# The fourth granule's x transposed by the DMA queue, and its FFN half moved back

## The chip, the core and the metric

The kernel runs on one core of a Trainium2 chip. The metric is the device time of one execution in microseconds; the median of several runs counts. Of the core's engines these notes speak of TensorE (PE; its weight loads are listed apart as PEld), VectorE (DVE), ScalarE (ACT), GpSimd (POOL) and SyncE (SP). SyncE computes nothing: it issues transfers to the core's 16 DMA engines, as GpSimd and ScalarE can too.

## What is computed

Attention over 4 batches, 8 heads, 768 positions and a head width of 64, with a window of 96 positions, 8 global positions and a bias by distance; then a feed-forward network with a scaled squared ReLU on the 3072 tokens of width 512.

```python
scores = q @ k.T / sqrt(64) - slope[h] * dist        # masked: kept if global or local
a = softmax(scores)
x = (a @ v), heads side by side                      # 3072 x 512
h = x @ w_in                                         # 3072 x 2048
g = s * relu(h) ** 2 + b
out = g @ w_out                                      # 3072 x 512
```

## The kernel before

The tokens are cut into twelve granules of 256 (three for each batch; j = 0 to 11), and each granule's attention into four units of two heads, so unit u belongs to granule u // 4. These notes count granules from 1 in words: the fourth is j = 3. (Where a number follows the word granule, as in granule 3, it is j.)

For a granule the work runs like this. GpSimd loads k, q and v (`load_granule`, L110 to L117; `load_qk`, `load_v`), cast to bf16 on the way. q and k are transposed: by TensorE for j = 0 to 3 (`qk_first`, `qk_block`, `qk_wide`), and by SyncE's queue, four transfers a granule, for j from 4 on (`qk_by_dma`, L356, issued at L360). `stage_S` makes a unit's scores on TensorE (L441), ScalarE takes the exponential (L450), VectorE multiplies by the mask (L457). `stage_A` multiplies by v (L495) and VectorE normalises into `xn` (L465, L466). Then `xn` has to be transposed into `xT`: `x_by_pe` (L583) does it with eight transposes of TensorE (L591) and two copies out of PSUM (L594), one of VectorE and one of ScalarE; `x_by_dma` (L596) does it with two transposing transfers of SyncE (L599). `finish_granule` (L950) takes the first for j below `X_PE`, which is 4. Behind it, it sends GpSimd a small copy that reads the end of `xT[j]` (`hold_loads`, L120, the copy is L122), and behind that copy the loads of granule j + 4: the loads wait in GpSimd's queue until `xT[j]` is there.

The FFN has two halves. The first (`p1_mm`, L612; matmuls at L619) takes two blocks of 128 hidden columns at a time, so eight groups `fp` of eight matmuls a granule; ScalarE applies the ReLU into `gT` (L629) and VectorE squares it (L632). The second half for the first four granules is `p2_mm` (L662; L667): for each of two output tiles `tb` of 128 tokens sixteen matmuls over the hidden blocks, which can be cut into ranges. `p2_out` adds the bias and stores through SyncE (L687). Later granules go in pairs through `product` (L819), a form with seven products for eight.

The order of the work on every engine is written by hand (`manual_schedule`): each engine takes its instructions in the order in which the lines run. Lines 1010 to 1143 are an opening, written line by line, up to granule 3's attention and x. From L1149 on the order comes from `step(s, c0, c1, c2)` (L959). Step s issues the transposes of granule j + 2 where its turn is (j = s // 2), emits the scores of step s + 1 with their exponentials and masks, then the list c0, the attention product of unit 2s, the list c1, that of unit 2s + 1, and the list c2; at a granule's second step it calls `finish_granule` after the first entry of c2. `flush` emits what was put off in `outs`. Step 8 and step 9 work on granule 4's attention and fill in FFN work: the second output tiles of granule 2 and the first half of granule 3 (`late_p1(3, ...)`). Step 10 begins the w_out tiles of granule 3.

In the opening, each head has a diagonal matrix (`diagonal`, L230), by which TensorE adds the bias of the first granules to the scores (L416, L517). ScalarE makes all eight (L232): four at L234, ahead of its cast of the first q (L260), and four at L1013, ahead of its copy of q's transposes (L331).

Of the kernel before, what the change touches and what calls it, by code (L numbers as in the profile page):

```python
# [17 lines left out]
def kernel(  # L18
# [13 lines left out]
    nc = tc.nc  # L32
    P = nc.NUM_PARTITIONS

    B, H, S, D = q.shape
# [9 lines left out]
    FC = DF // P  # L45
# [7 lines left out]
    QSCALE = 1.0 / float(D) ** 0.5  # L53
# [11 lines left out]

    ctx.enter_context(tc.manual_schedule())
    QK_PE = 4
    X_PE = 4
    LEAD = 4
    BIAS_PE = 2  # L70
    SHIFT = 6
# [112 lines left out]
    ident_bf = const.tile([P, P], BF16, name="ident_bf")  # L184
# [42 lines left out]
    slopes = [float(2.0 ** (-8.0 * (h + 1) / H)) for h in range(H)]  # L227
    diag = open_bf[:, 3 : 3 + H, :]

    def diagonal(hs):  # L230
        for h in hs:
            nc.scalar.activation(diag[:, h, :], ident_bf[:], ACT.Copy, scale=slopes[h] / QSCALE)  # L232

    diagonal(range(0, 4))  # L234

    tmpl = const.tile([P, H, 6, P], BF16, name="tmpl")

# [58 lines left out]
    def attach(b, lo, hi):  # L296

        kx = qk[b][0]
        nc.vector.tensor_copy(
            kx[:, lo:hi, :, P : P + NG],  # L300
            kx[:, 0, :, 0:NG].unsqueeze(1).to_broadcast((P, hi - lo, HP, NG)),
        )
# [53 lines left out]
    def qk_by_dma(j):  # L356
        b, g = divmod(j, NGR)
        for i in range(GB):
            for n in range(2):
                nc.sync.dma_start_transpose(  # L360
                    qk_of(b, n)[:, g * GB + i],
                    nat[j][:, n, i, :, :].rearrange("p h d -> p (h d)"),
                )
# [12 lines left out]
    def make_koff(j, blocks=range(GB)):  # L376
        b, g = divmod(j, NGR)
        if g == 0 or j >= SHIFT:
            return
        kx, ko = qk[b][0], koff_of(j)  # L380
        i0, n = blocks[0], len(blocks)
        lo = g * GB - 1 + i0
        nc.vector.tensor_copy(ko[:, i0 : i0 + n], kx[:, lo : lo + n, :, 0:P])
        nc.vector.tensor_copy(
            ko[:, i0 : i0 + n, :, 0:NG],
            kx[:, 0, :, 0:NG].unsqueeze(1).to_broadcast((P, n, HP, NG)),
        )
# [83 lines left out]
    def stage_A(u, pool=None):  # L471
        j, hp, b, g = unit(u)
        first = g == 0
        pt = st.pop(u)
        vn = vbuf[b % 2]
        if pool is None:
            av = ps_av.tile([P, GB, 2, VW], F32, name="ps_av", tag="av")
        else:
            av = pool.tile([P, GB, 2, VW], F32, name="ps_av2", tag="psh")
        if j not in xn:  # L480
            xn[j] = xpool.tile([P, GB, DM], BF16, name="xn", tag="xn")
        if first:
            dcol, ocol = ((0, 1), (None, 2)) if j < BIAS_PE else ((1, 2), (None, 0))
        else:
            dcol, ocol = (0, 3), (1, 2)
        for i in range(GB):
            for hi in range(2):
                h = 2 * hp + hi
                terms = [(dcol[i], vn[:, g * GB + i, h, 0 : D + 1])]
                if not first:  # L490
                    terms.append((ocol[i], voff_of(j)[:, i, h, 0 : D + 1]))
                elif i == 1:
                    terms.append((ocol[i], vn[:, 0, h, 0 : D + 1]))
                for n, (c, vv) in enumerate(terms):
                    nc.tensor.matmul(  # L495
                        av[:, i, hi, 0 : D + 1],
                        lhsT=pt[:, hi, c * P : (c + 1) * P],
                        rhs=vv,
                        start=(n == 0),
                        stop=(n == len(terms) - 1),  # L500
                    )
        normalize(
            xn[j][:, :, 2 * hp * D : (2 * hp + 2) * D].rearrange("p i (h d) -> p i h d", d=D), av
        )
# [78 lines left out]
    def x_by_pe(j, evac=(nc.vector.tensor_copy, nc.scalar.copy)):  # L583
        t = xT_tile(j)
        nk = KC // len(evac)
        for e, ev in enumerate(evac):
            ps = ps_h.tile([P, nk, GT], BF16, name="ps_x", tag="psh")
            for kc in range(nk):
                for i in range(GB):
                    c = (e * nk + kc) * P  # L590
                    nc.tensor.transpose(  # L591
                        ps[:, kc, i * P : (i + 1) * P], xn[j][:, i, c : c + P], ident_bf[:]
                    )
            ev(t[:, e * nk : (e + 1) * nk, :], ps[:])  # L594
# [6 lines left out]
    def g_of(j):  # L601

        if j // 2 not in gT:
            gT[j // 2] = gpool.tile([P, FC, 2 * GT], BF16, name="gT", tag="gT")
        return gT[j // 2][:, :, (j % 2) * GT : (j % 2 + 1) * GT]
# [6 lines left out]
    def p1_mm(j, fp):  # L612

        g = g_of(j)
        ps = ps_h.tile([P, 2, GT], F32, name="ps_1", tag="psh")
        for i in range(2):
            fc = 2 * fp + i
            for kc in range(KC):
                nc.tensor.matmul(  # L619
                    ps[:, i, :],  # L620
                    lhsT=w_in_bf[:, kc, fc * P : (fc + 1) * P],
                    rhs=xT[j][:, kc, :],
                    start=(kc == 0),
                    stop=(kc == KC - 1),
                )
        gs = g[:, 2 * fp : 2 * fp + 2, :]

        def relu():
            nc.scalar.activation(gs, ps[:], ACT.Relu)  # L629

        def square():
            nc.vector.tensor_tensor(gs, gs, gs, ALU.mult)  # L632

        return relu, square
# [27 lines left out]
    def p2_mm(j, tb, lo=0, hi=FC):  # L662
        if lo == 0:
            po_cur[j, tb] = ps_h.tile([P, DM], F32, name="ps_2", tag="psh")
        po = po_cur[j, tb]
        for fc in range(lo, hi):
            nc.tensor.matmul(  # L667
                po[:],
                lhsT=g_of(j)[:, fc, tb * P : (tb + 1) * P],
                rhs=w_out_bf[:, fc, :],  # L670
                start=(fc == 0),
                stop=(fc == FC - 1),
            )
# [34 lines left out]
    def moe_p2(j, tb):  # L708
        p2_mm(j, tb)
        outs.append(lambda: p2_out(j, tb))  # L710

    def flush():
        while outs:
            outs.pop(0)()
# [209 lines left out]
    def late_p1(j, fps):  # L924

        def go(fp):
            relu, square = p1_mm(j, fp)
            relu()
            outs.append(square)

        return [lambda fp=fp: go(fp) for fp in fps]

    p1 = {j: [lambda j=j, f=f: moe_p1(j, f) for f in range(FC // 2)] for j in range(NJ)}
    p2 = {j: [lambda j=j, t=t: moe_p2(j, t) for t in range(GB)] for j in range(NJ)}
    sums = [lambda i=i: wsum_add(i) for i in range(1, FC)]

    def run(cs):
        for c in cs:
            c()

    def scores(s):
        if s >= NU // 2:
            return []
        _, mms, posts = zip(*[stage_S(u) for u in (2 * s, 2 * s + 1)])
        for part in range(2):
            for mm in mms:
                mm(part)
        return posts[0] + posts[1]

    def finish_granule(j):  # L950
        if j < X_PE:
            x_by_pe(j)
        else:
            x_by_dma(j)
        if 6 <= j + LEAD < NJ:
            hold_loads(xT[j][0:1, 0, GT - 1 : GT])
            load_granule(j + LEAD)

    def step(s, c0, c1, c2, pool=None, pre=()):  # L959

        j = 2 * s // HP
        last = (2 * s + 2) % HP == 0
        if not last and j >= 4 and j + 2 < NJ:
            qk_by_dma(j + 2)
        posts = scores(s + 1)
        exps, masks = [c for i, c in enumerate(posts) if i % 2 == 0], posts[1::2]
        run(exps)
        run(pre)
        run(masks)
        run(c0)  # L970
        stage_A(2 * s)
        flush()
        if not last and j + 1 == QK_PE + 1:
            make_koff(j + 1)
        if not last and j % NGR == 0:
            attach(j // NGR, 1, NB)
        run(c1)
        stage_A(2 * s + 1, pool)
        flush()
        n = 2 if j < X_PE else 1  # L980
        run(c2[0:n])
        if last:
            finish_granule(j)
            if SHIFT < j + 2 < NJ:
                load_voff(j + 2)
        run(c2[n:])
        flush()
        if not last and j < SHIFT:
            make_voff(j + 1)
# [20 lines left out]
    warm(9, 4 * P)  # L1010
    cast_first(0, 0, cp)
    cast_first(0, 1, acp)
    diagonal(range(4, H))  # L1013
    qk_first(0, 0, cp)
    qk_first(0, 1, acp)
    open_bias((0, 1))
# [128 lines left out]
    def rest(j, tb):  # L1145
        p2_mm(j, tb, FC // 2, FC)
        outs.append(lambda: p2_out(j, tb))

    step(8, [lambda: rest(2, 0)] + late_p1(3, (0,)), late_p1(3, (1, 2)), late_p1(3, (3,)))  # L1149
    step(9, p2[2][1:2], late_p1(3, (4, 5)), late_p1(3, (6, 7)))  # L1150
    step(10, p2[3][0:1], [lambda: shifted_template(range(H))], late[0:2] + [bias_diff], ps_h)
    step(
        11,
# [97 lines left out]
```

The softmax here doesn't subtract the row's maximum and nothing guards it: scores larger than these inputs give would overflow.

## Time and profile before

| | us |
|---|---|
| median of 7 runs | 208.53 (208.43 to 209.25) |
| the profiled execution, its own time | 208.9 |
| its span, from the first to the last instruction | 207.1 |
| TensorE busy (its weight loads) | 201.5 (160.0) |
| VectorE, ScalarE, GpSimd busy | 159.8, 128.7, 70.5 |

The mean granted TensorE clock is 1.00. All times in the views below are microseconds from the start of the span. In the page's second part a row gives the busy share of 40 equal slices in tenths, so each digit stands for 5.2 us. A timeline line gives start, length, engine, line, operation, output<-inputs, shape and count; lengths of merged lines run from the first start to the last end, and a matmul's end lies behind the start of the next, since matmuls are pipelined. A queue line of a DMA view gives packets, megabytes and the time that the packets took as a share of 16 engines over the stretch asked for. The landing time of a transfer counts from the start of its issue.

### The profile page before, as it was taken

Reading aid. Unit: us, or ns where it says so; the run is one execution under the profiler, and the core shown is the slowest. Engines: PE = TensorE matmul, PEld = TensorE weight load, DVE = VectorE, ACT = ScalarE, POOL = GpSimd, SP = SyncE. Lnnn points to the kernel's source line nnn. Section 1 sums busy time; section 2 is a strip of 40 time slices with the busy share of each in tenths; the row PEclk is TensorE's granted clock in tenths of the full one; section 3 lists DMA queues with packets and bytes.
Section 4 is the critical chain, followed back from the end, with each engine's and each line's share of the span. In section 5 each row is a group of like instructions: output and inputs, shape, how many; then the busy total and the mean of one; then the engine's idle time right before and its main releaser. Section 6 shows DMA issues by size and latency. Waiting matters only on the chain.

```text
span 207.1 us, 5323 instructions
## 1 busy us (share of the span) xinstructions
PE 201.5 (97%) x2191; PEld 160.0 (77%) x2191; DVE 159.8 (77%) x336; ACT 128.7 (62%) x200; POOL 70.5 (34%) x90
## 2 busy tenths in 40 slices
PE   7899999999999999999999999999999999999993
PEld 2578884557867585878888898888888889888883
DVE  6686589877989856799799974699866696737974
ACT  4976669486976648686664595663695764476200
POOL 8986333899366300904700817200000000000000
DMA  5999999999999999999999999999460300240006
GB/s 162 173 179 200 207 208 177 155 153 129 131 144 125 156 149 222 120 228 231 130 196 141 137 142 215 171 195 87 53 205 3 94 12 0 57 149 0 0 9 197
DMA packets 110836, 28.17 MB, mean 136 GB/s; under 512 B 97852, under 2 KB 109308, under 8 KB 110812
## 3 DMA queue, kind: packets, MB, share of 16 engines
q0 software_dynamic: 76000, 13.11, 89.9%
q1 hardware_dynamic: 33612, 14.13, 38.9%
q10 hardware_dynamic: 1200, 0.59, 1.1%
q8 instruction: 17, 0.28, 0.5%
q14 instruction: 7, 0.06, 0.1%
HBM read 27.26 MB, written 6.29 MB: 162 GB/s over the span
## 4 chain that ended last, share of the span: by engine, by line
PE 74%; DMA 12%; POOL 5%; DVE 5%; ACT 1%; issue 1%; POOLq 0%
PE ps L619 33%; PE ps L819 24%; DMA nat<-in_q_dram 6%; PE ps L667 5%; DMA qx<-nat 4%; PE ps_s L441 4%; PE ps_av L495 4%; DVE wsum L645 4%; DMA first<-in_q_dram 2%; POOL nat L102 2%; POOL vb L108 1%; POOL nat L116 1%; DVE gT L632 1%; PE ps_s L517 1%; PE ps_s L532 1%
## 5 line engine op out<-in xcount | busy, mean ns | idle before, releaser
L619 PE MATMUL ps<-xT,w_in_bf 128*128 128x256 bf16 x768 | 90.3, 273 | 0.0
L629 ACT ACTIVATE gT<-ps 128x512 bf16<-128x512 f32 x96 | 55.7, 598 | 46.8 <-PE ps L619 46.6
L619 PEld LDWEIGHTS <-w_in_bf 128*128 128x128 bf16 x768 | 73.0, 98 | 9.4 <-DVE xT L594 0.2
L450 ACT ACTIVATE pt<-ps_s 128x1024 bf16<-128x1024 f32 (+1 forms) x44 | 39.3, 946 | 2.8 <-PE ps_s L441 2.7
L667 PE MATMUL ps<-w_out_bf,gT 128*128 128x512 bf16 x128 | 29.7, 380 | 0.0
L457 DVE TENSOR_TENSOR pt<-pt,tmpl 128x1024 bf16<-128x1024 bf16 (+1 forms) x40 | 24.6, 646 | 3.9 <-ACT pt L450 3.7
L819 PEld LDWEIGHTS <-gsum 128*128 128x128 bf16 x256 | 24.1, 98 | 3.8 <-DVE gsum L782 0.5
L108 POOL DMA_DIRECT2D vb<-in_v_dram x24 | 21.6, 914 | 6.6 <-DMA w_out_bf<-in_moe_w_out_dram 3.3
L793 DVE TENSOR_TENSOR gT<-gT 128x1024 bf16<-128x1024 bf16 x20 | 13.7, 687 | 11.7 <-ACT gT L629 11.7
L667 PEld LDWEIGHTS <-gT 128*128 128x128 bf16 x128 | 11.8, 98 | 13.0
L466 DVE TENSOR_TENSOR xn<-ps_av,rc 128x256 bf16<-128x256 f32 x48 | 20.4, 425 | 1.7
L819 PEld LDWEIGHTS <-gT 128*128 128x128 bf16 x200 | 18.6, 98 | 2.3
L465 DVE RECIPROCAL rc<-ps_av 128x4 f32<-128x4 f32 x48 | 8.6, 179 | 12.3 <-PE ps_av L495 10.3
L495 PEld LDWEIGHTS <-pt 128*128 128x128 bf16 x320 | 14.4, 97 | 2.7 <-DVE xn L466 0.7
L116 POOL DMA_DIRECT2D nat<-in_k_dram x16 | 14.2, 885 | 6.3 <-DMA nat<-in_k_dram 2.5
L632 DVE TENSOR_TENSOR gT<-gT 128x512 bf16<-128x512 bf16 x32 | 13.0, 421 | 3.7 <-ACT gT L629 3.3
L116 POOL DMA_DIRECT2D nat<-in_q_dram x16 | 14.2, 889 | 4.3 <-DMA nat<-in_q_dram 2.4
L495 PE MATMUL ps_av<-vb,pt 128*128 128x65 bf16 x208 | 15.4, 193 | 0.0
L819 PE MATMUL ps<-w_out_bf,gsum 128*128 128x256 bf16 x128 | 15.3, 273 | 0.0
L819 PE MATMUL ps<-wsub,gsum 128*128 128x256 bf16 x128 | 15.1, 273 | 0.0
L122 POOL COPY gate<-xT 1x1 bf16<-1x1 bf16 x6 | 2.1, 346 | 36.7 <-DMA xT<-xn 36.7
L819 PE MATMUL ps<-w_out_bf,gT 128*128 128x256 bf16 x120 | 13.9, 273 | 0.0
(111 smaller groups left out, 226.4 us busy)
## 6 DMA issues: line engine op xcount, KB each, us to landing
out_dram<-o_q SPq DMA_DIRECT2D x15, 256.0 KB, 2.4
vb<-in_v_dram POOLq DMA_DIRECT2D x24, 128.0 KB, 7.5
nat<-in_k_dram POOLq DMA_DIRECT2D x22, 128.0 KB, 7.0
nat<-in_q_dram POOLq DMA_DIRECT2D x22, 128.0 KB, 7.0
w_out_bf<-in_moe_w_out_dram POOLq DMA_DIRECT2D x4, 512.0 KB, 16.1
w_in_bf<-in_moe_w_in_dram POOLq DMA_DIRECT2D x4, 256.0 KB, 7.6
w_in_bf<-in_moe_w_in_dram POOLq DMA_DIRECT2D x2, 512.0 KB, 10.3
out_dram<-o_sb SPq DMA_DIRECT2D x4, 256.0 KB, 6.6
```

What stands on the lines that cost most here:

```text
L108: nc.gpsimd.dma_start(vbuf[b % 2][:, sb, :, 0:D], rows_of(v, b, sb))
L116: nc.gpsimd.dma_start(t[:, n, i, :, :], rows_of(srcs[n], b, sb))
L450: nc.scalar.activation(pt[:, :, 0:ncol], ps[:, :, 0:ncol], ACT.Exp, scale=QSCALE)
L457: nc.vector.tensor_tensor(pv, pv, m.rearrange("p h a c -> p h (a c)"), ALU.mult)
L466: nc.vector.tensor_tensor(dst, av[:, :, :, 0:D], rc[:].to_broadcast((P, 2, 2, D)), ALU.mult)
L495: nc.tensor.matmul(av[:, i, hi, 0 : D + 1], lhsT=pt[:, hi, c * P : (c + 1) * P], rhs=vv, start=(n == 0), stop=(n == len(terms) - 1),)
L619: nc.tensor.matmul(ps[:, i, :], lhsT=w_in_bf[:, kc, fc * P : (fc + 1) * P], rhs=xT[j][:, kc, :], start=(kc == 0), stop=(kc == KC - 1),)
L629: nc.scalar.activation(gs, ps[:], ACT.Relu)
L632: nc.vector.tensor_tensor(gs, gs, gs, ALU.mult)
L667: nc.tensor.matmul(po[:], lhsT=g_of(j)[:, fc, tb * P : (tb + 1) * P], rhs=w_out_bf[:, fc, :], start=(fc == 0), stop=(fc == FC - 1),)
L793: outs.append(lambda: nc.vector.tensor_tensor(gs, gs, gs, ALU.mult))
L819: nc.tensor.matmul(ps[:, tb, cs], lhsT=stat[:, fc, tb * P : (tb + 1) * P], rhs=mov[:, fc, cs], start=(fc == 0), stop=(fc == NH - 1),)
```

## The change

`X_PE` goes from 4 to 3, so that `finish_granule(3)` takes `x_by_dma`. The lists of steps 8 and 9 are dealt again: step 8 now holds both output tiles of granule 2, and the whole first half of granule 3 stands in step 9. And six diagonals are made by ScalarE at L234, the other two by VectorE in place of L1013.

```diff
-    X_PE = 4
+    X_PE = 3
...
-    diagonal(range(0, 4))
+    diagonal(range(0, 6))
...
     cast_first(0, 0, cp)
     cast_first(0, 1, acp)
-    diagonal(range(4, H))
+    for h in range(6, H):
+        nc.vector.tensor_scalar_mul(diag[:, h, :], ident_bf[:], slopes[h] / QSCALE)
     qk_first(0, 0, cp)
...
-    step(8, [lambda: rest(2, 0)] + late_p1(3, (0,)), late_p1(3, (1, 2)), late_p1(3, (3,)))
-    step(9, p2[2][1:2], late_p1(3, (4, 5)), late_p1(3, (6, 7)))
+    step(8, [lambda: rest(2, 0)], [lambda: p2_mm(2, 1, 0, FC // 2)], [lambda: rest(2, 1)])
+    step(9, late_p1(3, (0, 1, 2)), late_p1(3, (3, 4)), late_p1(3, (5, 6, 7)))
```

Instruction by instruction: TensorE loses the eight transposes of L591 between the last FFN group of granule 2 and the scores of step 8; ScalarE and VectorE lose one copy each (L594); SyncE gets two transposing transfers (L599) between the four of granule 5 and the four of granule 6; GpSimd's queue is the same, but its copy at L122 for granule 3 now waits for a transfer.

## The prediction

> **What bounds the kernel now.** First the page. TensorE is busy in every slice after the first, and the DMA engines are full nearly as long. q0 carries GpSimd's loads, q1 what SyncE issues; the two shares together pass 100%, since packets of both overlap on an engine.
>
> ```profile
> PE   7899999999999999999999999999999999999993
> DMA  5999999999999999999999999999460300240006
> q0 software_dynamic: 76000, 13.11, 89.9%
> q1 hardware_dynamic: 33612, 14.13, 38.9%
> ```
>
> So a part can be worth something on TensorE only where TensorE doesn't wait for a transfer. Next the chain of work that ended last, from 42 to 78 us (start, length, what):
>
> ```profile
> 48.41 11.55 DMA nat<-in_q_dram
> 59.96 0.02 issue
> 59.98 8.84 DMA qx<-nat
> 68.81 0.04 issue
> 68.86 0.57 PE ps_s L441 x14
> 69.42 3.56 PE ps L667 x16
> ```
>
> The scores of granule 5 (the matmuls of L441 in step 9) can't start before its q is loaded (59.96) and transposed by SyncE's queue (68.81). Neither date hangs on TensorE: GpSimd issues the loads one behind another from 36 to 51 us, as earlier ones land, and its queue never runs dry up to there. After 69.42 the chain is TensorE alone for the stretch that matters. The timeline of TensorE around the change (start, length, op, count):
>
> ```profile
> 58.79 0.61 PE L591 MATMUL ps_x<-ident_bf,xn 128*128 128x128 bf16 x8
> 59.34 0.40 PE L441 MATMUL ps_s<-qx,kx 64*128 64x128 bf16 x8
> ...
> 67.55 1.03 PE L619 MATMUL ps<-xT,w_in_bf 128*128 128x256 bf16 x8
> 68.52 0.69 PE L441 MATMUL ps_s<-qx,kx 64*128 64x128 bf16 x8
> ```
>
> The eight transposes of L591 hold TensorE for 59.34 - 58.79 = 0.55 us. At 68.52 TensorE is already early: eight score matmuls take 0.69 there and 0.40 at 59.34, so some 0.3 us of that is waiting for the 68.81. Whatever is saved before this point is waited out at this point.
>
> **What the parts cost, step by step.**
>
> *Opening.* ScalarE makes diagonals 4 to 7 from 5.65 on, and its copy of q's first transposes starts behind them, at 6.46. These transposes start at 5.80; k's, four as well, start at 5.29 and are copied at 5.73, 0.44 later, so the q copy could start at 6.24: 0.22 us earlier, and with it the first scores at 7.08. The two further diagonals that ScalarE makes at 3.17 cost 0.46 (0.91 for four), ahead of a cast that waits 1.05 us for its load. VectorE's two multiplies (nearest rows: 0.16 for the 128x128 comparison of L186, 0.20 for the copy of L193) lie in its idle 0.49 us ahead of 5.73. They cost 0 there, and would cost 0.2 to 0.4 at that spot without this cover. Gain 0.22 us at 7 us, and nothing at 68.86.
>
> *Transposes removed.* 0.55 us of TensorE. ScalarE's copy of L594 (0.58) and VectorE's (0.42) go too; ScalarE's stands right before the exponentials that TensorE waits 0.42 us for at 62.15, so up to 0.42 more.
>
> *Order of steps 8 and 9.* Between 62.7 and 68.5 four groups of FFN matmuls (16 of them take 1.75 us in the chain, so four groups of eight 3.50) give way to sixteen w_out matmuls (3.56, from 69.42): +0.06. TensorE so comes to the scores at 68.52 - 0.55 - 0.22 - (0 to 0.42) + 0.06, that is 67.4 to 67.8, and stands until 68.86 as before. Sum up to the end of these scores (69.42): **0**, with the savings as a longer wait.
>
> *The wait that is added.* Behind these scores TensorE's next work was the second output tile of granule 2 (data long there). In the changed order it is the first FFN matmul of granule 3, which reads xT; and xT now comes by two transposes on SyncE's queue, each of a 128x512 tile like the four of a granule's q and k. Their place there, from the timeline of SP:
>
> ```profile
> 56.63 1.19 SPq L360 DMA_TRANSPOSE qx<-nat  x1
> 57.91 1.24 SPq L360 DMA_TRANSPOSE kx<-nat  x1
> 59.98 1.26 SPq L360 DMA_TRANSPOSE qx<-nat  x1
> 65.25 1.19 SPq L360 DMA_TRANSPOSE kx<-nat  x1
> ```
>
> They are emitted ahead of the 65.25 one, and granule 3's attention is normalised by 58.35, so SyncE issues them in its idle stretch at about 61.3 and 62.6. When they land is the disputed cost, and two rows bound it. By latency: the DMA view asked for single issues gives 8.0, 8.6 and 8.8 us to landing at 53.32, 56.63 and 59.98, and 6.9 and 8.5 at 66.61 and 68.19; 62.6 + 6.9 to 8.8 is 69.5 to 71.4. By order in q1: the transposes issued at 56.63 and 59.98 landed at 65.2 and 68.8, two in 3.6 us, 1.8 each. The packets from 65.8 to 67.8, and from 68 to 69.5, say why:
>
> ```profile
> q0 software_dynamic: 1407, 0.18, 138.8%
> q1 hardware_dynamic: 535, 0.13, 51.4%
> ...
> q0 software_dynamic: 1816, 0.23, 251.1%
> ```
>
> A transpose is some 520 packets on q1 (520 to 540 in each of four such bursts). It passes beside q0 in 1.5 to 1.9 us, burst by burst, and the burst ending at 67.7 is the one that lands at 68.81. q0 is held by granule 6's loads until its last one lands at 70.7, whether granule 7's follow or not. So xT's two bursts come behind 67.7 and take 1.3 us (nearest: 490 packets from 69.5 to 71.2) to 1.8 each, and land 1.1 later: 71.4 to 72.4. Lowest end: spaced as the transposes issued at 79.83 and 81.24, when q0 is empty (3.5 and 2.5 us to landing: 83.3 and 83.7, so 0.4 each), 68.8 + 0.8 = 69.6. Highest: 62.6 + 10.1, the latency of that last load, 72.7. I take 71.6, near the burst rows, because they are of the same queue in the same microseconds. TensorE then stands for 71.6 - 69.42 = **2.2 us** (0.2 to 3.3), and nothing else runs: queued behind the waiting matmul are all eight FFN groups, both attention products of step 9 and the w_out tiles of granule 3; ScalarE and VectorE wait for these.
>
> The Trainium skill, "DMA: Bandwidth & Descriptors", Specifications and Anatomy of one DMA, speaks against this wait: it gives a transfer issued from SyncE some 0.6 us to its first byte and about 2 us of fixed cost. By it xT would land near 65 and the sum would be 0; the rows of this stretch (6.9 to 8.8 us) disagree, those of the emptied queue (2.5) agree.
>
> *Behind the wait.* Step 9 holds 64 FFN matmuls and two attention products: 7.00 + 0.48 = 7.48, against 7.54 before (3.56 + 0.48 + 3.50). ScalarE has eight copies of 0.60 there and two exponentials done during the wait: no bound. The exponentials, SyncE's output stores and granule 6's transposes (behind xT's in q1, so up to 2 x 1.8 later than 77.7; read at 81.49 + 2.2) keep their cover. GpSimd's gate for granule 7's loads (L122, 61.41) reads this xT and so opens at 71.6, 10 us later; six issues of 0.88 and 7 us to landing end near 84, the transposes of granule 7 by 92, and they are read at 93.87 + 2.2. Granule 4's x, landed at 82.3 and first read at 83.67, is issued near 78.5 and may meet those loads: 5.1 us gives 83.6 and 8.8 gives 87.3, against a read at 85.9, so 0 to 1.4; I take 0, because q0 then has half its load behind it. Behind this TensorE has no stop of 0.2 us or more, so nothing takes the delay back.
>
> Sum: 0 + 2.2 + 0 on the profiled execution's 208.9 (a span of 207.1 and 1.8 around it), that is 211.1. That execution is 0.37 above the median of 208.53, so the forecast for the median is **210.7**.
>
> **Rivals.**
>
> *In time, and granule 5's transposes earlier: faster.* One mechanism: a lighter q1 and q0 between 61 and 68. For it: xT's own transposes take a median of 5.0 us over the run, and 62.6 + 5.0 is 67.6. From 63.0 to 63.8 the DMA engines nearly stop, while GpSimd issues granule 7's second load; the gate moves that load away, so this stop may go and the 68.81 may become 68.0. TensorE is there at 67.4 to 67.8, so 0.8 us is won: 208.53 - 0.8 = **207.7**. It decides from xT landing before 68.6, when the scores then end. Against: other stops, as near 54.5 and 74.5, have no such issue in common, and every transpose issued from 53 to 70 took 6.9 us or more.
>
> *In time, nothing else moves:* xT lands before 69.42, the scores stay at 68.86. Change 0, **208.5**. This is also where the change wouldn't do what it is made for: TensorE is rid of 0.55 us and stands that much longer.
>
> *Late, and TensorE slow behind it.* TensorE would stand from 67.6 to 71.6 but for 0.56 us. At the start of the kernel matmuls of 512 columns come 0.43 us apart up to 4.2 us, later 0.22 (3.56 for sixteen). If the wait brings that rate back for as long as at the start, 3 us, half of it is lost: 1.5 more, **212.2**. For it only that opening; the clock column of the windows view shows 1.00 throughout, also over the start, so it can't decide.
>
> The Trainium skill, "TensorE: Matmul & The Clock Gate", Part 1, has the clock halved after an idle window of about 3.4 us. A stand of 2.2 us doesn't fill such a window, so by this page the sum stays at 2.2; no row of this trace has such a gap.
>
> **How the numbers follow.** Forecast (late by 0.2 to 3.3 us) 0.73; faster rival 0.11; unchanged 0.08; slow clock 0.08. The forecast's bounds are 208.7 and 211.8 (208.53 + 0.2 and + 3.3); up to 1.4 for granule 4's x may come on top. The range goes down to 208.3 to take in the unchanged case and up to 212.6, which takes in 0.8 of that 1.4 and the slow clock's centre; it leaves out the faster rival and single ends. Faster by over 0.2% (about what a measurement here can tell from no change) has 0.11, within 0.2% 0.08, slower 0.81.
>
> **What would show it.** Right: no L591 near 59; SyncE's two L599 at about 61.3 and 62.6 with 8 us or more to landing; the scores of step 9 at 68.9; then the first L619 of granule 3 idle some 2 us with the xT transfer as its releaser; the gate of L122 as late as that; later stages shifted by one amount. Wrong: xT landing below 6.8 us after its issue; the chain passing through something other than xT there; a stop at the read of granule 4's x or of granule 7's q; a further shift behind 80 us.

## The result, and the profile after

The changed kernel takes **211.82 us** (median of 12 executions, 210.51 to 213.26) against 208.63 for the kernel before in the same rounds (30 executions, 208.32 to 209.25). The ratio is **1.0153, 95% interval 1.0132 to 1.0173**: slower by 1.5%. The forecast was 210.7 in a range of 208.3 to 212.6. Here and below, a ratio leaves out executions that took over 1.5% more than the fastest of the same kernel.

The twelve executions fall into two groups by the granted TensorE clock. Seven have a mean clock of 1.00 over the span (210.51 to 211.97, the middle one 211.11), five have 0.992 (212.74 to 213.26, the middle one 212.85). Every execution of the kernel before whose clock is on record had 0.997 or more. The profiled execution of the changed kernel is one of the five: 212.81, with a span of 211.0. Of the parts of its page (engines, their clock, the DMA engines and the two queues, as before) these rows answer to those shown of before:

```profile
PE   7999999999999599999999999999999999999993
...
PEclk9999999999999799999999999999999999999999
DMA  6999999999999999999999999999260210240005
...
q0 software_dynamic: 76000, 13.11, 86.2%
q1 hardware_dynamic: 34700, 14.39, 39.9%
```

The 14th slice (68.6 to 73.8 us) is new on both rows of TensorE: it is idle nearly half of the time, and its clock is lower. q1 has 1088 packets more, the two transposes of xT. Next the chain of work that ended last, from 57.8 to 77.7 us:

```profile
58.60 0.62 DVE ko L383
59.23 0.02 issue
59.25 0.19 DVE ko L384
59.44 0.05 issue
59.49 0.40 PE ps_s L441 x8
...
62.15 0.57 PE ps_s L441 x16
62.72 1.16 SPq L599
63.88 0.05 issue
63.94 7.47 DMA xT<-xn
71.41 0.05 issue
71.45 4.23 PE ps L619 x24
75.69 0.24 PE ps_av L495 x8
75.93 1.75 PE ps L619 x16
```

Before, the chain went here through granule 5's q (`qx<-nat`, landed at 68.81) and then stayed on TensorE. Now it goes through xT: the second transpose is issued at 63.94 and lands 7.47 us later. Two further things are new. VectorE's `ko` copies (the shifted keys of granule 4) stand at 59 us, and the 24 matmuls of L619 behind xT take 4.23 us, where the 16 after them take 1.75 (24 would be 2.63). The timeline of SyncE, and that of TensorE around the wait (in brackets the idle time ahead, and what ended it):

```profile
59.57 1.26 SPq L360 DMA_TRANSPOSE qx<-nat  x1
60.93 4.30 SPq L599 DMA_TRANSPOSE xT<-xn  x2
65.33 1.22 SPq L360 DMA_TRANSPOSE kx<-nat  x1
```

```profile
58.81 0.40 PE L441 MATMUL ps_s<-qx,kx 64*128 64x128 bf16 x8
59.49 0.40 PE L441 MATMUL ps_s<-qx,ko 64*128 64x128 bf16 x8 [0.29 <-DVE ko L384]
...
68.41 0.40 PE L441 MATMUL ps_s<-qx,kx 64*128 64x128 bf16 x8
68.64 0.39 PE L441 MATMUL ps_s<-qx,ko 64*128 64x128 bf16 x8
71.45 4.23 PE L619 MATMUL ps<-xT,w_in_bf 128*128 128x256 bf16 x24 [2.43 <-DMA xT<-xn]
```

The scores of step 9 no longer wait: their eight matmuls take 0.40, and granule 5's q had landed at 68.02. TensorE then stands for 2.43 us. Its work behind these scores began at 69.42 before and begins at 71.45 now: **2.03 us later**. The windows view of the changed kernel, cut at the points where the clock changes (length, TensorE busy with count, granted clock, DMA share, GB/s):

```profile
67.61:71.02 3.41, 1.42 (x21) 1.00 1.76 159
71.02:74.43 3.41, 2.98 (x15) 0.50 1.35 227
74.43:77.84 3.41, 3.41 (x44) 1.00 1.80 177
```

For 3.41 us the clock is at half. TensorE works in 2.98 of these and so loses half of that, **1.5 us**. The third loss is at the very end. These are SyncE's waits behind the last matmuls (waiter, releaser, total us, times, longest), first before, then after:

```profile
SPq L1246 <- DMA out_dram<-o_last: 0.7, 3, 0.3
...
SPq L1246 <- DMA out_dram<-o_q: 0.4, 1, 0.4
```

```profile
SPq L1247 <- DMA out_dram<-o_last: 1.4, 2, 1.3
```

From the start of the last matmul to the end of the span it is 3.46 us before and 3.81 after: **0.35 us**, though the same stores go out at the same distance behind the matmuls. SyncE ends the program by waiting for its transfers, a semaphore at a time and in a fixed order. With two more transfers on SyncE's queue the last stores end on semaphores that are waited for early; by the trace seven further waits of about 0.06 us then follow the last landing, where there was one.

The three add up to 2.03 + 1.5 + 0.35 = 3.9, and the spans of the two profiled executions differ by 211.0 - 207.1 = 3.9.

### The profile page after: what moved, and what is told of

It is laid out like the page before. It is cut to its first block, busy times and chain, and to the rows that moved or that the text cites. A ratio compares the mean times of both kernels' runs of the same rounds, so it can differ in the third digit from the quotient of the medians.

```text
span 211.0 us, 5308 instructions
## 1 busy us (share of the span) xinstructions
PE 203.1 (96%) x2183; PEld 160.5 (76%) x2183; DVE 160.3 (76%) x337; ACT 128.0 (61%) x197; POOL 69.8 (33%) x90
## 4 chain that ended last, share of the span: by engine, by line
PE 86%; DMA 5%; DVE 4%; ACT 2%; SPq 1%; issue 0%
PE ps L619 37%; PE ps L819 23%; PE ps L667 11%; PE ps_s L441 5%; PE ps_av L495 4%; DMA xT<-xn 4%; DMA first<-in_k_dram 2%; PE ps_t L351 1%; PE ps_s L517 1%; DVE xn L466 1%; ACT pt L450 1%; ACT gT L629 1%; DVE gT L632 1%; PE ps_s L532 1%; DVE nat L260 1%; PE ps_av L558 1%
## 5 line engine op out<-in xcount | busy, mean ns | idle before, releaser
L619 PE MATMUL ps<-xT,w_in_bf 128*128 128x256 bf16 x768 | 91.4, 275 | 2.4 <-DMA xT<-xn 2.4
L619 PEld LDWEIGHTS <-w_in_bf 128*128 128x128 bf16 x768 | 73.8, 99 | 12.5 <-DMA xT<-xn 2.6
L122 POOL COPY gate<-xT 1x1 bf16<-1x1 bf16 x6 | 1.8, 304 | 42.7 <-DMA xT<-xn 42.7
```

What stands on the lines that cost most here:

```text
L619: nc.tensor.matmul(ps[:, i, :], lhsT=w_in_bf[:, kc, fc * P : (fc + 1) * P], rhs=xT[j][:, kc, :], start=(kc == 0), stop=(kc == KC - 1),)
```

## The experiments

**The theory.** xT lands at 71.4 because its two transposes pass on the DMA engines behind granule 5's and beside granule 6's loads; TensorE stands for it with nothing else queued. Where the clock halves, the standing has caused that. **The rivals.** The new order of steps 8 and 9 or the diagonals cost the time themselves; a transpose of SyncE has such a latency anyway, with or without the loads; the gate of L122, now 10 us later, costs it; the lower clock has another cause than the stop.

**The order without the transfer.** The changed kernel with x by TensorE again:

```diff
-    X_PE = 3
+    X_PE = 4
```

> The changed kernel, but with granule 3's x transposed by TensorE as before: the new deal of steps 8 and 9 and the diagonals alone. Transfer theory (the loss is TensorE's wait for xT, which lands at 71.4, with the half clock behind it in some executions): xT is there by 60.4, so no wait in step 9 beyond that for granule 5's q; 208.2 to 208.8, the time of the kernel before. Order theory (the new deal itself costs, by a longer run of FFN groups in step 9 that ScalarE and VectorE can't follow): 210 or more.

Measured: 208.68, ratio 1.0003 (0.9992 to 1.0014), clock 0.997 or more in all twelve executions. The new lists and the diagonals cost nothing and bring nothing; the whole loss hangs on xT's way.

**The diagonals alone,** in the kernel before:

```diff
-    diagonal(range(0, 4))
+    diagonal(range(0, 6))
...
-    diagonal(range(4, H))
+    for h in range(6, H):
+        nc.vector.tensor_scalar_mul(diag[:, h, :], ident_bf[:], slopes[h] / QSCALE)
```

> The kernel before with the diagonals alone made apart (six by ScalarE at once, two by VectorE). Theory: ScalarE's copy of q's transposes starts at 6.2 to 6.35 in place of 6.46 and TensorE runs 0.1 to 0.2 us early from there, all of it waited out at the scores of granule 5, whose q lands at 68.5 to 68.9 as before: within 0.1% of before. Rival (TensorE's own work sets the end from the start): 0.1 to 0.2 us faster.

Measured: 208.65, ratio 1.0005 (0.9996 to 1.0014). The first scores come at 7.14 in this run's trace and at 6.99 in the changed kernel's, against 7.08 before; these dates hang on the clock of the opening too (see the account below). At granule 5's scores nothing of a gain is left: 68.58 here against 68.52.

**The transfer without the order.** The kernel before with nothing else changed than:

```diff
-    X_PE = 4
+    X_PE = 3
```

> The kernel before with X_PE = 3 alone: granule 3's x by SyncE's queue, steps 8 and 9 and the diagonals as before. Transfer theory: the first FFN group of granule 3 then stands behind the first output tile of granule 2, at about 64, while xT lands at 71.4 as in the changed kernel; TensorE stands 7 us there, and behind it has four groups and two attention products less done, so the scores of granule 5 no longer wait: the time is that of before plus some 7 (215 to 216), and with the half clock behind so long a stand 216.5 to 218. Against the theory that the order of steps 8 and 9 gains nothing for the transfer: 211 to 212.

Measured: 217.68, ratio 1.0438 (1.0409 to 1.0468), clock 0.976 to 0.984. With the FFN groups still in step 8, TensorE meets xT some 5 us earlier:

```profile
62.53 1.90 PE L667 MATMUL ps<-w_out_bf,gT 128*128 128x512 bf16 x8
...
70.99 1.89 PE L619 MATMUL ps<-xT,w_in_bf 128*128 128x256 bf16 x8 [6.56 <-DMA xT<-xn]
```

xT lands at 70.95, near the 71.41 of the changed kernel, whatever TensorE does meanwhile: the date belongs to the DMA engines. (In the five traces with this order on SyncE's queue and granule 6's loads beside it, xT lands at 70.59 to 71.41.) The new order is what keeps the loss at 3 us rather than 9.

**The stop filled.** Eleven matmuls, whose result nothing reads, ahead of the first FFN group of granule 3:

```diff
+    def fill(n):
+        ps = ps_h.tile([P, 4 * P], F32, name="ps_w", tag="psh")
+        for i in range(n):
+            nc.tensor.matmul(ps[:], lhsT=w_out_bf[:, 0, 0:P], rhs=w_out_bf[:, 0, :], start=True, stop=True)
...
-    step(9, late_p1(3, (0, 1, 2)), ...
+    step(9, [lambda: fill(11)] + late_p1(3, (0, 1, 2)), ...
```

> The changed kernel with eleven matmuls of 512 columns on data long there (their result is read by nothing) between the scores of step 9 and the first FFN group of granule 3: about 11 x 0.22 = 2.4 us of work in a wait of 2.6. Transfer theory with the clock as a consequence of the wait: xT still lands at about 71.4, the time is that of the changed kernel's executions at a clock of 1.00 (210.5 to 212.0, their middle 211.1), and no execution shows 0.992. If the low clock is not from the wait: again about 5 of 12 executions at 0.992 and 212.7 to 213.3.

Measured: 211.2 (211.06 to 211.41), ratio 1.0124 (1.0108 to 1.0139), clock 0.997 or more in all five executions. The timeline of TensorE, and the window that answers to the halved one:

```profile
68.89 2.55 PE L1155 MATMUL ps_w<-w_out_bf 128*128 128x512 bf16 x11
71.28 2.78 PE L619 MATMUL ps<-xT,w_in_bf 128*128 128x256 bf16 x24
```

```profile
67.61:71.02 3.41, 3.17 (x28) 1.00 1.78 159
71.02:74.43 3.41, 3.41 (x37) 1.00 1.35 233
```

With TensorE busy all the while the 24 matmuls take 2.78 instead of 4.23, and no execution is in the upper group. The lower clock comes from the stop, and what the late xT costs at full clock is 211.2 - 208.61 = 2.6 us. From 94 us on, this kernel's matmuls are 1.96 behind those of before, one by one up to the last; with the 0.35 of the end on top that is 2.3, the difference of the two spans (209.4 and 207.1; that execution of before took 0.3 more than its median).

**The loads of granule 6 held back too.** In the changed kernel only granule 7's loads wait for xT of granule 3; here both do, so that q0 is empty while xT passes:

```diff
-        if 6 <= j + LEAD < NJ:
+        if 7 <= j + LEAD < NJ:
             hold_loads(xT[j][0:1, 0, GT - 1 : GT])
+            if j == 3:
+                load_granule(6)
             load_granule(j + LEAD)
```

> The changed kernel with granule 6's loads also held until xT of granule 3 is there (they stand behind the same small copy of GpSimd, ahead of granule 7's). Contention theory (xT lands late because q0 shares the engines with granule 6's loads, packet by packet): q0 is empty from about 62, granule 5's transposes and xT's land at 2.5 to 4 us from issue, xT by 67; no wait in step 9; granule 6's loads land some 73, its transposes by 79, ahead of their reading at 81.5; 207.7 to 208.5. Rival 1 (the transposes are slow by themselves, or by their order in q1): xT again at 70 or later, 210.5 or more. Rival 2 (granule 6 becomes late): a new wait of 1 to 3 us at the scores of step 11, 209.5 to 211.5.

Measured: 212.73, ratio 1.0208 (1.0173 to 1.0243); four of six executions at clock 1.00 (211.88 to 213.03). This run separates the two theories of xT's latency. The DMA view from 62.45 to 62.6 us gives xT's second transpose with its time to landing:

```profile
xT<-xn SPq DMA_TRANSPOSE x1, 2.5
```

It lands at 64.9 instead of 71.4, and step 9 has no wait. So it was the loads, and not the latency of a transpose. But the time expected of it was wrong: the loads of two granules now run together behind 65 us, and others are late by them:

```profile
69.07 2.79 PE L619 MATMUL ps<-xT,w_in_bf 128*128 128x256 bf16 x24
...
82.26 0.46 PE L441 MATMUL ps_s<-qx,kx 64*128 64x128 bf16 x10 [0.77 <-DMA qx<-nat]
...
86.54 1.91 PE L619 MATMUL ps<-xT,w_in_bf 128*128 128x256 bf16 x16 [1.99 <-DMA xT<-xn]
```

Granule 6's q and granule 4's x now make TensorE stop, for 0.8 and 2.0 us. The DMA engines are full; an empty queue for one transfer is paid by the next.

**Granule 7's loads not behind xT.** The gate of L122 reads granule 2's xT, so the loads start where they did before:

```diff
-            hold_loads(xT[j][0:1, 0, GT - 1 : GT])
+            hold_loads(xT[2 if j == 3 else j][0:1, 0, GT - 1 : GT])
```

> The changed kernel with the small copy of GpSimd ahead of granule 7's loads reading granule 2's xT, which is there since 51, in place of granule 3's: the loads go out at 61 as before the change. Theory: the late gate costs nothing, and q0 is full with granule 6's loads until xT has landed either way; xT at 71 to 72, time 210.5 to 213.3, as the changed kernel. Rival (the gate that moved 10 us is part of the loss, through granule 7's data or granule 4's x): 0.5 us or more faster than the changed kernel at equal clock.

Measured: 213.29, ratio 1.0224 (1.0204 to 1.0243), four of five executions at clock 0.992 (213.17 to 213.59) and one at 1.00 (210.84). In its profiled execution, the one at clock 1.00, xT lands at 70.87 and the first matmul of L619 waits 1.41. The later gate is not where the loss comes from: taking it away leaves the stop.

**`ko` made earlier.** The line `make_koff(4)` moves ahead of granule 2's FFN groups, so that VectorE's copies (L383, L384) are done before the scores of step 8 need them:

```diff
     qk_by_dma(5)
+    make_koff(4)
     r0, q0 = p1_mm(2, 5)
...
-    make_koff(4)
```

> The changed kernel with VectorE's copy of granule 4's shifted keys (make_koff(4)) emitted before the attention of units 14 and 15 and not behind it. In the changed kernel TensorE waits 0.45 us for that copy at 59.49, where the eight transposes stood. Theory: that wait goes, TensorE comes to the scores of step 9 at about 68.0 in place of 68.4, and then stands longer for xT, which lands as late as before; 211 to 212.2, no gain over the changed kernel, with the wait for xT some 0.4 longer. Rival (TensorE's own work sets the end, not xT): 0.4 faster than the changed kernel.

Measured: 212.49, ratio 1.0152 (1.011 to 1.0194); two executions at clock 1.00 with 210.44 and 210.53, three at 0.991 to 0.992 (212.2 to 213.1), and one at 0.984 (214.18). The wait at 59.49 is gone and the scores of step 9 come at 68.06 in place of 68.41. The stop still ends when xT lands, which in this trace is at 70.59. The two at full clock are 0.6 below the changed kernel's middle, but that kernel spreads over 210.51 to 211.97, so two executions don't tell the rival's gain of 0.4 from none. Its windows tell something else: TensorE is at work again from 70.63, and the clock falls behind that.

```profile
70.80:71.00 0.20, 0.20 (x4) 1.00 1.48 205
71.00:71.20 0.20, 0.20 (x4) 0.61 1.37 230
...
74.40:74.60 0.20, 0.20 (x3) 0.85 0.89 348
```

**xT ahead of granule 5's second block** on SyncE's queue:

```diff
-    qk_by_dma(5)
+    qk_by_dma(5, [0])
...
     finish_granule(3)
+    qk_by_dma(5, [1])
```

> The changed kernel with xT's two transposes issued ahead of the transposes of granule 5's second block (SyncE's queue: first block of granule 5, xT, second block). Queue theory (q1 passes about one transpose in 1.5 us beside the loads, in order of issue, and there are simply two more of them before 72): xT takes the places at 66.4 and 68.0, granule 5's q lands at 71 to 71.5; the wait goes from xT to the scores of step 9, and as these 0.55 us now stand behind the wait too, the time is that of the changed kernel plus 0.5: 211 to 213.7. Latency theory (each transpose needs 7 to 9 us by itself, whatever is ahead): granule 5's q lands at 70 and xT at 67, 209.5 to 211.

Measured: 213.24, ratio 1.0182 (1.0142 to 1.0222); one execution at clock 1.00 (211.2), the others at 0.984 to 0.992. xT's two transposes land at 66.57 and 68.06, as the order in the queue lets one expect, and granule 5's q at 71.53 in their place:

```profile
68.40 0.23 PE L441 MATMUL ps_s<-qx,kx 64*128 64x128 bf16 x2
71.58 0.50 PE L441 MATMUL ps_s<-qx,kx 64*128 64x128 bf16 x6 [2.94 <-DMA qx<-nat]
72.44 3.87 PE L619 MATMUL ps<-xT,w_in_bf 128*128 128x256 bf16 x24
```

The queue has so much room up to 71.5, and who stands last in it waits. Only work that needs neither can fill the hole.

**FFN work put where xT is there already.** The queue's order of the last run, four of granule 3's eight FFN groups at the end of step 8 (ahead of granule 5's scores), and `ko` early:

```diff
-    step(8, [lambda: rest(2, 0)], [lambda: p2_mm(2, 1, 0, FC // 2)], [lambda: rest(2, 1)])
-    step(9, late_p1(3, (0, 1, 2)), late_p1(3, (3, 4)), late_p1(3, (5, 6, 7)))
+    step(8, [lambda: rest(2, 0)], [lambda: p2_mm(2, 1, 0, FC // 2)], [lambda: rest(2, 1)] + late_p1(3, (0, 1, 2, 3)))
+    step(9, late_p1(3, (4,)), late_p1(3, (5,)), late_p1(3, (6, 7)))
```

> A version built on the queue theory: xT's transposes ahead of the second block of granule 5 as in the run e_first, four FFN groups of granule 3 behind the second output tile in step 8, so that they cover the time until granule 5's q lands, and VectorE's copy of granule 4's shifted keys early. Queue theory: xT lands at 68 and is read at 68.0, granule 5's q lands at 71.5 and its scores stand at 71.5: no stop over 0.3 us between 58 and 80, the eight transposes (0.55) and the wait of before (0.28) are won: 207.8 to 208.4, that is 0.1 to 0.4% below before. If it isn't so, granule 5's q lands later than 72 and the scores wait: 209 or more.

Measured: 210.81, ratio 1.0112 (1.0086 to 1.0139), all executions at clock 1.00. Two stops remain, 1.09 us for xT ahead of 68.88 and 1.84 ahead of 77.04 for VectorE, which had granule 5's v copies (73.55 to 75.2) and masks (75.16 to 76.4) ahead of normalising the unit that frees the buffer:

```profile
68.88 3.67 PE L619 MATMUL ps<-xT,w_in_bf 128*128 128x256 bf16 x32 [1.09 <-DMA xT<-xn]
...
77.04 0.20 PE L495 MATMUL ps_av<-vb,pt 128*128 128x65 bf16 x1 [1.84 <-DVE xn L466]
```

**Step 9 by hand.** The queue's order again; now the scores of granule 5 go behind four FFN groups and both attention products of granule 4:

```python
run(late_p1(3, (0, 1)))
stage_A(18); flush()
run(late_p1(3, (2,)))
stage_A(19); flush()
run(late_p1(3, (3,)))
finish_granule(4); flush()
run(scores(10))
run(late_p1(3, (4, 5, 6, 7))); flush()
```

> x of granule 3 by SyncE's queue ahead of granule 5's second block, as in the run e_first, and step 9 written out by hand: two FFN groups, attention of unit 18, a group, attention of unit 19, a group, granule 4's x, and only then the scores of granule 5, then the last four groups. Queue theory: xT lands at 68.1 and is read at 68.4; granule 5's q lands at 71.5 to 72.1 and its scores stand at 72.4; VectorE has the attentions of step 9 done ahead of the masks, which stood in the way in the run v_first. No stop over 0.3 us; 0.53 of TensorE's time won: 207.9 to 208.4, 0.1 to 0.35% below before. If the scores, exponentials and masks are late for step 10 so: a stop of up to 1 us at the attention of unit 20, 208.5 to 209.5.

Measured: 208.87, ratio 1.0019 (1.0007 to 1.0031). The wait for xT is gone: the first L619 starts at 68.32 right behind the matmuls before it, and granule 5's scores at 72.44. Its last matmul comes at 203.58, before's at 203.65; the 0.35 at the end is more than what it lies behind. The same step 9 with x by TensorE:

```diff
-    X_PE = 3
+    X_PE = 4
```

> The same hand-written step 9, with granule 3's x by TensorE and the order of SyncE's queue as before the change. The part that comes from the order alone: the scores of granule 5 stand 4 us behind the landing of its q, so the wait of 0.28 us goes, the eight transposes stay: 208.3 to 208.5, 0 to 0.2% below before. If this is as fast as v_step9, the DMA transposes win nothing.

Measured: 208.66, ratio 1.0000 (0.9991 to 1.0009). With xT by transfer the median is 0.21 longer and the end of the program 0.35, so leaving the eight transposes out of TensorE gained some 0.14 us up to the last matmul, not 0.55. One stop in the trace with xT by transfer shows where such a gain goes:

```profile
59.31 0.34 PE L441 MATMUL ps_s<-qx,kx 64*128 64x128 bf16 x6 [0.54 <-DMA qx<-nat]
```

The eight transposes stand in front of granule 4's scores and cover what lands or is copied meanwhile; without them TensorE waits for it instead. What that is differs from trace to trace: here it is granule 4's q, which landed at 59.27 (57.98 to 58.71 in the other traces), in the changed kernel it was `ko`. A second wait, 0.25 us at 83.62, is for granule 4's x: its second transpose is issued at 74.69 beside granule 7's loads and takes 8.8 us to landing. One trace for each kernel doesn't show what share of the 0.4 each such wait takes on the average.

**The end shortened.** The last kernel but one with the two small loads of s and b moved from SyncE's queue to GpSimd's, so that SyncE issues as many transfers as before the change:

```diff
-        nc.sync.dma_start(s_bc[:], moe_s.to_broadcast((P, 1)))
-        nc.sync.dma_start(b_bc[:], moe_b.to_broadcast((P, 1)))
+        nc.gpsimd.dma_start(s_bc[:], moe_s.to_broadcast((P, 1)))
+        nc.gpsimd.dma_start(b_bc[:], moe_b.to_broadcast((P, 1)))
```

(It starts from the kernel with step 9 by hand and xT by transfer.)

> The kernel of v_step9 with the two small loads of the scalars (L167, L168) issued by GpSimd in place of SyncE, so that SyncE's queue carries as many transfers as in the kernel before. Theory (the closing waits of SyncE are longer by 0.35 us because two more transfers of SyncE turn the order of the semaphores on which the last stores end): the last matmul stays near 203.6 us, the span ends 3.46 us behind it in place of 3.81, and the time is 208.5, 0.17 per cent under v_step9 and 0 to 0.1 per cent under the kernel before. Rival (the longer end comes from something else in the order with the fourth granule's x by transfer, such as the position of the last stores): the end stays at 3.81 and the time at 208.87. A third way: GpSimd's two further issues of 0.9 us hold its loads back, and the last matmul comes later.

Measured: 209.15 (208.65 to 212.03), ratio 1.0013 (0.9993 to 1.0032): the time expected, 208.5, did not come. In its profiled execution the mechanism holds. The last store is issued at 203.57 and the span ends at 207.1, 3.5 us later; with the loads on SyncE it is 203.46 and 207.4, 3.9. SyncE's waits are those of before again:

```profile
SPq L1259 <- DMA out_dram<-o_last: 0.6, 3, 0.3
SPq L1259 <- DMA out_dram<-o_q: 0.4, 1, 0.4
```

But GpSimd's first load of granule 6 goes out at 53.84 instead of 50.94, behind the two small ones and the gate, and the time of single executions varies more (spans of 206.9 to 207.8, and one of 210.3). Where the longer ones lose it isn't shown, since only one execution has a trace. None of the versions is faster than the kernel before.

## Why the prediction was right, and where it was off

| step of the prediction | forecast | measured |
|---|---|---|
| TensorE at granule 5's scores | 67.4 to 67.8 | 68.41 |
| granule 5's q landed | 68.81 | 68.02 |
| xT issued | 61.3 and 62.6 | 60.93 and 63.94 |
| xT landed | 71.6 (69.6 to 72.7) | 71.41 (70.59 to 71.04 in four other traces) |
| work behind the scores begins later by | 2.2 | 2.03 |
| gate of L122 | 10 us later, costs 0 | 10 us later, costs 0 |
| granule 4's x | 0 (0 to 1.4) | landed 83.29, no wait |
| given back behind 80 us | nothing | nothing |
| the end of the program | not a step | +0.35 |
| clock at half | 1.5, with a chance of 0.08 | 1.5, in 5 of 12 executions |

*The added wait* was the right mechanism, at the right place and nearly of the right size. The working that carried it was the passage in bursts on q1 beside q0: 71.6 against 71.41. The shape of the packets as a bound is borne out by the held loads, where the same transpose takes 2.5 us with q0 empty, and by the turned order, where xT and granule 5's q change dates. The Trainium skill, "DMA: Bandwidth & Descriptors", Anatomy of one DMA, gives about 2 us of fixed cost for a transfer on GpSimd's path; the prediction took it for one of SyncE. The 2.5 us of SyncE's transfer are near it, the 7.5 us of the same transfer beside the loads are not, and it was these that counted.

*The savings* were priced at zero for a reason that was half right. The forecast had them waited out at granule 5's q. TensorE came 0.53 us early to granule 4's scores (58.81 against 59.34), but the transposes had hidden VectorE's `ko` copies: the second half of these scores starts at 59.49 against 59.57, so 0.45 was gone at once. The earlier exponentials (0 to 0.42 in the forecast) brought nothing, 62.09 against 62.15. That is why TensorE stood at granule 5's scores at 68.41 and not at 67.4 to 67.8. There q had landed, so the 0.3 us of waiting fell away too; the scores ended 0.4 early, and that was waited out at xT, a stop of 2.43 for a delay of 2.03. That the removed instructions covered something was not looked for.

*The opening* was sized at 0.22, and the pair of traces compared, 6.99 against 7.08, doesn't measure it. Matmuls of 512 columns come 0.43 us apart up to 4.58 in the changed kernel's trace, whose record of the clock begins with its rise at 6.17; in that of before the closer spacing begins behind 4.15. In three traces with the new diagonals and a rise by 4.8 us (x by TensorE in the new order, the filled stop, step 9 by hand) the first scores come at 6.60 to 6.67, 0.41 to 0.48 early. Nothing hangs on it: the diagonals alone leave the time where it was.

*The faster rival* had xT in time, and the pause of the DMA engines at 63.0 to 63.8 gone with GpSimd's load there. GpSimd issues nothing from 60.9 to 71.46 in the changed kernel, and the pause is there all the same (63.2 to 64.0, the three low digits in the DMA view's row from 61 to 71 us below, 0.25 us each); its reason is refuted. Granule 5's q did come 0.8 us earlier, as that rival had it, but this was worth nothing, because xT came at 71.41 and not by 68.6. Nor is it shown to come from the change: in the four traces with granule 3's x by TensorE this q lands at 67.96, 67.97, 68.51 and 68.81, in the five with it by transfer behind this q at 66.89 to 68.35. The wait of 0.3 us at 68.52, on which the prediction built, belongs to the trace of before: with the diagonals alone the same eight matmuls take 0.40.

```profile
DMA  9999999990119999999999999999999999999999
```

*The slow clock* is the step that failed: a chance of 0.08 for what came in 5 of 12 executions. The forecast argued from an idle stretch that must fill the whole of a window, and from no such gap in the trace of before. The clock column of before, 1.00 throughout, could not warn it: that trace keeps no record of the clock. The runs show a window that is only part idle. The clock was at half from 71.02 to 74.43 in the changed kernel, from 71.04 to 74.46 with `ko` early and from 71.27 to 74.69 with the queue turned, 3.41 us each time, and behind the 6.56 us stop from 69.46 to 76.29, twice that. In each of the thirteen traces that record the clock, any two of its changes lie a whole multiple of 3.413 us apart (1, 2, 19, 40, 41, 59 or 60 times). So it is set at the ends of stretches of 3.41 us that follow one another, and these can be placed in a trace whose clock stayed, too. Here are three stretches of the run with the 6.56 us stop, then the last full one of the run with step 9 by hand, at the end of its matmuls:

```profile
62.63:66.05 3.42, 1.80 (x8) 1.00 2.45 106
66.05:69.46 3.41, 0.00 (x0) 1.00 1.68 156
69.46:72.87 3.41, 1.88 (x12) 0.50 1.68 158
...
202.15:205.56 3.41, 1.65 (x23) 1.00 0.81 265
```

The clock fell to half behind stretches in which TensorE was busy for 0.00, 0.77 (queue turned), 1.42 (changed kernel) and 1.46 us (`ko` early); with `ko` early TensorE was at work again for 0.4 us by then. It stayed at 1.00 behind the stretch with 1.80, behind that with 1.65 at the end of the program, and behind every one with more: 2.01 around xT with granule 7's loads let go, 2.32 with FFN work put earlier, 3.18 with the stop filled. Between 1.46 and 1.65 of 3.41 us the traces leave it open; a clock already at half stayed there behind 1.88. The stretches begin elsewhere in each execution, so the same stop can fall into one of them or be parted between two. An estimate from these numbers: a stop of 1.95 to 2.43 us (the two traced with the clock at half behind the same order) puts at least 3.41 - 1.46 = 1.95 us of idle time into one stretch in 43 to 57 of 100 placings; hit were 5 of 12 executions, and 4 of 6 with `ko` early. The mean clock of 0.992 in all five fits one such stretch: 3.41 us at half in 211 are 0.008. The Trainium skill, "TensorE: Matmul & The Clock Gate", Part 1, has such a free-running window of about 3.4 us, and the length agrees; it speaks of an idle window, and here one that was busy for 1.46 of 3.41 us was enough.

*The sum.* At full clock the forecast was 2.17 above the median of before; measured are 2.48 (the middle of seven executions) and 2.6 with the stop filled. The term that was missing is the 0.35 of the end. The rest up to the median of 211.82 is the second group: with five of twelve executions 1.74 longer, the median lies at the upper edge of the first group. That it lies inside the range is in part luck: with seven of twelve in the second group it would have been 212.7 or more, above the 212.6. Why the seven at full clock spread over 1.5 us, where before spreads over 0.9, stays open.

## What to carry to other kernels

Work taken off the busiest engine is worth what is next late behind it: list what the removed instructions were covering (a copy on another engine, a landing) and follow each date before counting the saving. A landing on a full queue, read from one trace, is one of a spread: granule 5's q moved by 0.85 us among four traces in which its way was the same. Price a transfer by rows of the same queue in the same microseconds, with the loads that run beside it, not by its time on an empty queue; where the DMA engines are full, changing the order chooses who waits, and only work that needs neither transfer fills the hole. And a stop of TensorE of 2 us can cost 1.5 us more than itself when the clock halves behind it, which some executions show and others don't, so look at several.

## What the runs showed of the hardware

- The clock was at half for 3.41 us, or 6.82, and changed only at whole multiples of 3.413 us from its other changes. It fell behind stretches of 3.41 us in which TensorE was busy for 0.00 to 1.46, and stayed at 1.00 behind those with 1.65 or more; filling the stop with matmuls that nothing reads kept it at 0.997 or more in five of five executions.
- In the opening, matmuls of 512 columns came 0.43 us apart up to the first rise of the clock and 0.23 behind it; the rise came at 4.18 us (step 9 by hand) to 7.14 (loads held).
- A transposing transfer of a 128x512 tile landed 2.5 us after its issue with GpSimd's queue empty, and 7.5 us after it beside a granule's loads.
- SyncE itself is held by such issues: the two of granule 3's xT took it 4.30 us in the changed kernel and 3.09 with the loads held back, the two of granule 4's 2.52. Most single ones take 1.2 to 1.9; the longest stood where the DMA engines nearly stop, as the first of the 4.30 us (2.95, from 60.93).
- Two transfers more on SyncE's queue lengthened the end of the program by 0.35 us, with the last stores issued at the same distance from the last matmul; two fewer took that away again.
